# Adding the residual of row tiles 0 to 7 with accumulating stores from GpSimd onto rows that already hold x

## The chip, the cores and the metric

The kernel runs on one core of one Trainium2 chip. The time is the device time of one execution in microseconds, as the median of several runs. A profile is one further execution with the hardware profiler on; its span runs from the first to the last instruction.

The core's engines run their own instruction queues and wait for one another through semaphores: TensorE (PE, matmuls into the PSUM banks), VectorE (DVE), ScalarE (ACT), GpSimd (POOL) and SyncE (SP, which here issues every DMA). DMAs move data between the device memory (HBM) and the on-chip memory (SBUF).

## What is computed

One transformer block on x of 2048 rows and 512 columns in bfloat16, with the attention and the gated MLP side by side:

```
xn  = layernorm(x)
q, k, v = split(xn @ wqkv)                  # 32 heads of 16
att: each row attends to itself and rows -2, -4, ... -14   (8 positions, dilation 2)
A   = softmax(q.k / 4) . v  ->  @ wo
B   = (gelu(xn @ w_gate) * (xn @ w_up)) @ w_down            # inner width 1376
out = x + A + B
```

The last line matters here: x, the residual, is added to the sum of the two branches.

## The kernel before

The rows are cut into 4 blocks (b = 0 to 3) of 512 rows, and each block into 4 row tiles of 128 rows, so that there are 16 row tiles t. Names carry these numbers: `pr2_1` is work of block 2, `fe7` work of row tile 7.

For each block, in the order of the data:

- The row tiles are loaded (`ld_x`), normalised (`norm`) and transposed into xnT: block 0 by PE, the others by DMA transposes from SP (`trx`).
- PE computes q, k and v (`mm<b>_<q|k|v>_<group>`, L1009; block 0's q and k in smaller pieces) and ACT evicts them (`ev`).
- DVE multiplies q with the eight shifted views of k (`pr`, 128 x 4096 elements each) and adds pairs (`pa`). PE sums over the head's columns (`er`, L1085). DVE and ACT do the softmax (`d1`, `d2`, `exp`, `d4` to `d6`). The probabilities go to HBM and come back replicated over partitions (`ss`, then `sl` into PT, L1176). DVE multiplies them with v (`pv`), adds (`pw`) and writes the attention's output (`pz`, L1199).
- PE computes the gate and up products (`fg`, `fu`, L1217), ACT applies gelu (`gelu`) and evicts (`uev`), DVE multiplies the two (`h`).
- For each row tile, PE accumulates attention output times Wo and MLP inner times Wd in one PSUM bank (`acc`, L1302).

Then comes the part that is changed. For row tiles 0 to 13, ACT evicts the bank into one of four slots of the buffer OB (`fe`, L1335), DVE adds x in place from one of two slots of XR (`fin`, L1340), and SP stores the slot to the output (`sto`, L1353). SP loads XR beforehand (`ldxr`, L1288). Row tiles 14 and 15 are cut into two and three pieces, and DVE adds x straight from PSUM (L1346).

The order on every engine is written out by hand: `ORDER` holds one list of task names per engine. `schedule` assigns the buffer slots along these lists, with a model of durations, and `assign_sync` derives the semaphore waits. No engine leaves its list: an instruction that waits holds everything behind it. A slot of OB is free when the DMA that read it has landed, and the next `fe` that takes that slot waits for it on ACT. The last stores on SP are preceded by waits for all earlier DMAs. GpSimd has only constants to write, and four small powers for the normalisation (`sq8` to `sq14`, L832).

Of the kernel before, what the change touches and what calls it, by code (L numbers as in the profile page):

```python
# [12 lines left out]
    DMA_ISSUE=0.48,  # L13
    DMA_FIXED=2.0,
# [5 lines left out]
    DRAIN=0.1,  # L20
# [115 lines left out]
class Graph:  # L136
# [70 lines left out]
    def schedule(self, orders, params=None):  # L207
        prm = dict(PARAMS)
# [58 lines left out]
        for _ in range(len(self.tasks)):  # L267
# [23 lines left out]
            elif t.eng == "pe":  # L291
                sw = 0.0
                if t.mode is not None:
                    if pe_mode not in (None, t.mode):
                        sw = prm["PE_MODE_SWITCH"]
                    pe_mode = t.mode
                t.end = est + sw + pe_clock.run(est, t.dur, t.util)
                t.done = t.end + prm["PE_DRAIN"]
            else:
                t.end = est + t.dur  # L300
                t.done = t.end + prm["DRAIN"]
                if t.eng == "act" and t.table is not None:
                    act_table = t.table
# [13 lines left out]
    def assign_sync(self, cnt_sems, dma_sems):  # L317
        order = self.order
        for e in ("pe", "act", "dve", "pool"):
            for i, t in enumerate(order[e]):  # L320
                t.seq = i + 1
                t.sem = cnt_sems[e]
                t.val = i + 1
        dcount = [0] * len(dma_sems)
        dlast = [None] * len(dma_sems)
        k = 0
        for t in order["sp"]:
# [6 lines left out]
            dlast[si] = t  # L334
        self.dma_totals = [(dma_sems[i], dcount[i]) for i in range(len(dma_sems)) if dcount[i] > 0]
        know = {e: {} for e in ENGS}
        allt = sorted((t for t in self.tasks if not t.dropped), key=lambda t: (t.start, t.idx))
        for t in allt:
            K = know[t.eng]
            deps = list(t.deps)  # L340
            if t.eng == "sp" and t.prev_on_sem is not None:
                deps.append(t.prev_on_sem)
# [21 lines left out]
    def emit_engine(self, eng_name, e):  # L364
# [7 lines left out]
        for t in self.order[eng_name]:  # L372
# [10 lines left out]
            ins.then_inc(t.sem, 16 if eng_name == "sp" else 1)  # L383
# [5 lines left out]
    def report(self):  # L389
# [30 lines left out]
    "act":  # L420
        "c_tbl sx1 sq0 negm1 sxx1 sq1 evx0_0 evx0_1 evq0_0 sq2 evq0_1 evk0_0 evx1_0 sq3 evk0_1 bnst8 evx1_1 "
        "bnst9 evq0_2 sq6 evk0_2 evq0_3 evk0_3 ve8 evv0_0_0 sq4 vp8 bnag8 bnag9 va8 gelu0_0 evv0_2_0 "
        "evv0_3_0 bnst10 gelu0_1 bnst11 uev0_2 gelu0_3 vb8 gelu0_4 uev0_1 uev0_3 ve10 gelu0_5 uev0_4 uev0_0 "
        "uev0_5 gelu0_2 halo1 vp10 gelu0_7 bnag10 bnag11 evq1_0_0 evk1_0_0 evv0_1_0 evq1_1_0 evk1_1_0 "
        "gelu0_6 exp0 sub11 evq1_3_0 evk1_3_0 evq1_2_0 va10 uev0_7 uev1_0 uev0_10c uev0_6 sub9 vb10 sub8 "
        "uev1_1 evk1_2_0 norm9 uev0_10b gelu1_1 gelu1_0 norm8 gelu0_8 evv1_0_0 gelu1_2 sub10 uev0_8 bnst12 "
        "gelu0_9 norm11 uev1_2 uev0_9 norm10 evv1_2_0 gelu1_4 gelu1_3 uev1_3 evv1_1_0 uev1_4 uev1_5 uev0_10a "
        "bnst13 gelu1_5 gelu0_10 uev1_6 evk2_1_0 evv1_3_0 evk2_0_0 ve12 vp12 gelu1_7 bnag12 evq2_0_0 gelu1_6 "
        "evq2_1_0 uev1_10b bnag13 uev1_10c halv1 evk2_2_0 evq2_2_0 halo2 exp1 bnst14 sub12 bnst15 uev1_7 "
        "va12 ve14 vb12 uev1_10a vp14 bnag14 evk2_3_0 bnag15 evq2_3_0 evv2_1_0 va14 vb14 fe1 fe2 sub14 "  # L430
        "gelu2_0 evv2_2_0 halo3 gelu1_10 sub15 uev2_0 norm12 sub13 evv2_0_0 evv2_3_0 norm13 fe0 norm15 fe3 "
        "norm14 gelu1_8 gelu2_1 gelu1_9 uev2_1 uev1_8 uev2_2 uev1_9 uev2_3 gelu2_2 evk3_2_0 evk3_1_0 "
        "uev2_10b gelu2_3 exp2 evq3_1_0 evk3_3_0 evq3_2_0 evq3_0_0 halv2 evk3_0_0 uev2_10c evq3_3_0 uev2_4 "
        "uev2_10a gelu2_10 gelu3_1 uev3_0 gelu3_0 fe7 evv3_0_0 gelu2_5 gelu3_3 evv3_1_0 uev2_5 uev3_1 fe5 "
        "gelu2_4 gelu3_2 uev3_10c halv3 evv3_3_0 uev3_2 fe4 fe6 uev3_3 uev3_10b exp3 gelu3_5 uev2_6 gelu3_4 "
        "gelu2_7 uev2_7 uev2_8 gelu3_6 gelu2_6 evv3_2_0 gelu3_7 uev3_4 gelu2_8 gelu2_9 uev2_9 uev3_10a "
        "uev3_7 uev3_5 uev3_6 gelu3_10 fe10 gelu3_8 gelu3_9 uev3_9 fe9 uev3_8 fe8 fe11 fe13 fe12",
    "dve":
        "c_wdz bnst0 bnag0 sub0 rstd0 norm0 mean1 sub1 evy0_0 rstd1 norm1 evy0_1 bnst2 bnag2 sub2 rstd2 "
        "norm2 bnst3 bnag3 sub3 rstd3 norm3 bnst7 bnst6 bnst5 bnag6 bnag7 bnst4 bnag5 sub7 rstd6 bnag4 sub6 "  # L440
        "norm7 sub4 sub5 norm6 pr0_2 pr0_0 pr0_3 rstd4 pr0_1 norm4 norm5 pa0_1 pa0_0 h0_0 h0_1 h0_2 mask "
        "d1_0 d2_0 pr1_0 pr1_1 d4a_0 d4b_0 d4c_0 d5_0 rstd8 d6_0 pr1_3 pa1_0 pr1_2 h0_3 pa1_1 pv0_1 rstd10 "
        "pv0_3 h0_4 pv0_0 h1_1 pv0_2 pw0_1 h0_10 pw0_2 d1_1 pw0_3 d2_1 pz0 pr2_2 d4a_1 pr2_0 d4b_1 h1_3 "
# [12 lines left out]
        "ss0_1 ldxr2 sl0_1 sl0_3 sl0_2 trx4_0 sl0_0 trx4_1 trx5_1 trx5_0 ss1_2 ss1_3 ss1_1 ss1_0 sl1_1 sl1_3 "
        "sl1_0 sl1_2 ldxr3 trx6_0 trx6_1 trx7_1 trx7_0 sto3 sto1 ldxr0 ldxr7 ss2_1 ss2_2 ss2_3 ss2_0 sl2_0 "
        "sl2_3 sl2_2 sto0 sl2_1 sto2 ldxr5 ldxr4 sto5 ss3_0 ss3_1 ss3_2 ss3_3 ldxr10 sl3_3 sl3_0 sl3_2 sl3_1 "
        "ldxr6 sto4 sto6 ldxr8 ldxr9 sto9 ldxr11 ldxr14 sto8 sto7 sto10 ldxr13 sto11 sto14_0 sto14_1 ldxr15 "
        "ldxr12 sto13 sto15_0 sto15_1 sto12 sto15_2",  # L460
# [20 lines left out]
def bass_parallel_sum__sliding_local_dilated__glu_gated_geglu__prompt_kernel(nc, A_x, A_wqkv, A_wo, B_x, B_w_gate, B_w_up, B_w_down, out, dbg=None, cfg=None):  # L481
# [28 lines left out]
    PPOW = cfg.get("PPOW", 4)  # L510
    FIN2 = cfg.get("FIN2", tuple(range(14)))
# [12 lines left out]
    with contextlib.ExitStack() as es:  # L524
# [56 lines left out]
        cnt = {e: es.enter_context(nc.semaphore("cnt_" + e)) for e in ("pe", "act", "dve", "pool")}  # L581
        dsems = [es.enter_context(nc.semaphore("dma%d" % i)) for i in range(NDMASEM)]
# [360 lines left out]
        for b in range(NB):  # L943
# [338 lines left out]

            for ti in range(4):
                t = 4 * b + ti
                it_xr = Item("xr%d" % t, P_xr, "xr")

                def mk_xr(t=t, it=it_xr):
                    return lambda e: e.dma_start(XR[:, it.slot, :], x2[128 * t:128 * t + 128, :])  # L1288
                t_xr = G.task("sp", "ldxr%d" % t, 0, mk_xr(), wr=[it_xr], prio=base + 58, nbytes=128 * 1024)
                G.order_after(t_xr, t_of["gelu%d_5" % b])  # L1290
                cparts = TAIL_SPLIT.get(t, [(0, 512)])
                for ci, (c0, c1) in enumerate(cparts):
# [40 lines left out]
                    if t in FIN2:  # L1333
# [4 lines left out]

                        def mk_fin(itx=it_xr, ito=it_ob):
# [14 lines left out]
                    G.task("sp", "sto" + sfx, 0, mk_so(), rd=[it_ob], wr=[(I_out, (t, ci))], prio=base + 62,  # L1354
# [11 lines left out]
        G.assign_sync(cnt, dsems)  # L1366
# [50 lines left out]
```

## Time and profile before

| what | value |
| --- | --- |
| median of 5 runs | 184.15 us (183.92 to 184.55) |
| the profiled execution: time, span | 183.92 us, 182.1 us |
| matmuls of 512 columns (L1217), four in a row | 0.86 us |
| DVE, 128 x 4096 elements (L1040) | 2284 ns, 16 of them |
| DVE, `fin` (L1340) | 14 of them, 5.7 us in all |
| ACT, `fe` (L1335) | 14 of them, 600 ns each |
| POOL, power (L832) | 4 of them, 866 to 6880 ns |
| `ldxr` (L1288): issue to landing, median | 2.2 us, 128 KB each |
| `sto` (L1353) of 128 KB: issue to landing, median | 2.0 us |

The time of an execution is its span and the little that lies around it, here 1.8 us. An engine's busy time and share of the span are given by the profile's first part; "idle before" is the time an engine stood still ahead of an instruction, with what ended it. Lines are given as L and a number, and belong to the kernel before. A duration in the profile can be longer than the step to the next instruction of the same engine, as neighbours overlap at their ends.

### The profile page before, as it was taken

To read this page: it belongs to the slowest core of one execution; us is meant where nothing else is said; L and a number is where in the kernel's file an instruction comes from. 1 tells how busy PE (TensorE), PEld (TensorE's weight loads), DVE (VectorE), ACT (ScalarE), POOL (GpSimd) and SP (SyncE) were. 2 spreads that over 40 slices of the span, in tenths; PEclk is the share of its full clock that TensorE was granted. 3 is DMA by queue.
4 is the path that set the end of the run, shared out by engine and by line. 5 is a ranking of instruction groups with operands and counts; after the bars stand their busy time and mean duration, and the time that the engine had idled before them with its cause. 6 is when DMAs were issued, how large, how long until landed. Compare 5 with 4: busy or idle time off the path is not lost.

```text
span 182.1 us, 2773 instructions
## 1 busy us (share of the span) xinstructions
PE 177.5 (97%) x1051; PEld 90.4 (50%) x1068; DVE 169.6 (93%) x172; ACT 128.4 (71%) x258; POOL 15.7 (9%) x23
## 2 busy tenths in 40 slices
PE   8999999999999999999999999999999999999994
PEld 2895444544444544444444544444444444444664
DVE  3779999999999999999999999999999999999922
ACT  5789977999998999997795977437449664234011
POOL 6000049004200000131000000000000000000000
PEclk9999999999999999999999999999999999999999
DMA  4999925932562000003861020127200355022433
GB/s 137 363 376 380 118 31 128 363 110 59 193 126 58 0 0 0 4 17 81 250 60 30 25 61 0 32 59 237 79 0 0 95 152 191 0 86 59 146 94 107
DMA packets 26220, 19.60 MB, mean 108 GB/s; under 512 B 13824, under 2 KB 23008, under 8 KB 26208
## 3 DMA queue, kind: packets, MB, share of 16 engines
q1 hardware_dynamic: 26208, 19.44, 37.7%
q8 instruction: 8, 0.13, 0.3%
q14 instruction: 4, 0.03, 0.1%
HBM read 14.71 MB, written 3.15 MB: 98 GB/s over the span
## 4 chain that ended last, share of the span: by engine, by line
PE 95%; DMA 1%; issue 1%; ACT 1%; DVE 0%; SPq 0%; DVEq 0%
PE PS L1217 38%; PE PS L1302 28%; PE PS L1009 19%; PE PS L959 4%; PE PS L1256 2%; PE PS L1085 2%; PE PS L1078 1%; DMA XIN<-in_A_x_dram 1%; PE PS L899 1%; ACT KT L986 0%; ACT xnT L919 0%; PE PS L678 0%; SPq L731 0%; DVE XIN L873 0%; DVE OB L1346 0%
## 5 line engine op out<-in xcount | busy, mean ns | idle before, releaser
L1302 PE MATMUL PS<-Wd,HT 128*128 128x512 bf16 (+2 forms) x206 | 40.7, 345 | 0.3 <-issue 0.2
L1217 PE MATMUL PS<-xnT,Wg 128*128 128x512 bf16 x156 | 39.0, 379 | 0.2
L1217 PE MATMUL PS<-xnT,Wu 128*128 128x512 bf16 x156 | 38.9, 379 | 0.2
L1009 PE MATMUL PS<-xnT,Wqkv 128*128 128x512 bf16 x155 | 37.2, 379 | 0.4 <-issue 0.2
L1184 DVE TENSOR_TENSOR UNI<-VN,PT 128x4096 f16<-128x4096 bf16 x16 | 36.2, 2281 | 0.0
L1040 DVE TENSOR_TENSOR UNI<-QT,KT 128x4096 f16<-128x4096 bf16 x16 | 36.1, 2284 | 0.0
L1302 PEld LDWEIGHTS PS<-Wd,HT 128*128 128x128 bf16 x209 | 19.5, 98 | 19.2 <-issue 0.4
L1234 ACT ACTIVATE UU<-PS 128x512 bf16<-128x512 f32 x40 | 23.1, 599 | 6.6 <-PE PS L1217 6.3
L1193 DVE TENSOR_TENSOR UNI<-UNI 128x4096 f16<-128x4096 f16 x12 | 27.4, 2284 | 0.0
L1227 ACT ACTIVATE GG<-PS 128x512 bf16<-128x512 f32 x40 | 22.9, 601 | 5.6 <-DVE HT L1241 5.5
L1009 PEld LDWEIGHTS PS<-xnT,Wqkv 128*128 128x128 bf16 x160 | 17.9, 113 | 16.9 <-issue 0.8
L1217 PEld LDWEIGHTS PS<-xnT,Wu 128*128 128x128 bf16 x160 | 15.6, 98 | 19.0 <-ACT XIN L853 0.4
L1217 PEld LDWEIGHTS PS<-xnT,Wg 128*128 128x128 bf16 x160 | 15.7, 98 | 18.7
L1335 ACT ACTIVATE OB<-PS 128x512 bf16<-128x512 f32 x14 | 8.3, 600 | 17.3 <-PE PS L1302 15.1
L832 POOL TENSOR_TENSOR sq<-ve,mhalf 128x2 bf16<-128x2 f32 x4 | 12.8, 3200 | 66.0 <-ACT ve L828 66.0
L1053 DVE TENSOR_TENSOR UNI<-UNI 128x4096 f16<-128x4096 f16 x8 | 18.2, 2282 | 0.0
L1302 PE MATMUL PS<-Wo,OT 128*128 128x512 bf16 (+2 forms) x75 | 16.4, 345 | 0.1
L1020 ACT ACTIVATE VN<-PS 128x512 bf16<-128x512 f32 x16 | 9.3, 596 | 6.5 <-PE PS L1009 6.5
L1241 DVE TENSOR_TENSOR HT<-GG,UU 128x1024 bf16<-128x1024 bf16 x20 | 13.5, 682 | 0.0
L1302 PEld LDWEIGHTS PS<-Wo,OT 128*128 128x128 bf16 x76 | 7.1, 98 | 6.6 <-issue 0.3
L1272 ACT ACTIVATE UT<-PS 64x256 bf16<-64x256 f32 (+1 forms) x12 | 5.4, 448 | 6.7 <-PE PS L1256 3.9
L959 PE MATMUL PS<-xnT,Wqkv 128*128 128x128 bf16 x128 | 8.0, 219 | 0.1
(85 smaller groups left out, 159.1 us busy)
## 6 DMA issues: line engine op xcount, KB each, us to landing
PT<-pt_scratch SPq DMA_DIRECT2D x16, 256.0 KB, 4.1
XR<-in_A_x_dram SPq DMA_DIRECT2D x16, 128.0 KB, 2.2
out_dram<-OB SPq DMA_DIRECT2D x14, 128.0 KB, 2.0
Wqkv<-in_A_wqkv_dram SPq DMA_DIRECT2D x3, 512.0 KB, 4.8
XIN<-in_A_x_dram SPq DMA_DIRECT2D x6, 256.0 KB, 6.3
Wg<-in_B_w_gate_dram SPq DMA_DIRECT2D x1, 1280.0 KB, 8.8
Wu<-in_B_w_up_dram SPq DMA_DIRECT2D x1, 1280.0 KB, 11.7
Wd<-in_B_w_down_dram SPq DMA_DIRECT2D x1, 1280.0 KB, 6.3
```

Of the source, the lines that this page charges most:

```text
L832: "pool", "sq%d" % t, 7.0, lambda e, t=t, n=n: e.tensor_tensor(out=sq[:, t:t + n], in0=ve[:, t:t + n], in1=mhalf[:, 0:n], op=ALU.pow),
L959: ins = e.matmul(PS[:, 512 * it.slot + 128 * g:512 * it.slot + 128 * g + 128], lhsT=wcols(which, kt, g), rhs=xnT[:, itx.slot, kt, t * 128: ...
L1009: ins = e.matmul(PS[:, 512 * it.slot:512 * it.slot + 512], lhsT=wcols(which, kt, g), rhs=xnT[:, itx.slot, kt, :], start=(kt == 0), stop=(k ...
L1040: return lambda e: e.tensor_tensor(out=UNI[:, it.slot, :, :], in0=bass.AP(QT, (itq.slot * 4 + g) * 512, [[NQT * 4 * 512, 128], [0, 8], [1, ...
L1053: return lambda e: e.tensor_tensor(out=UNI[:, i0.slot, :, :], in0=UNI[:, i0.slot, :, :], in1=UNI[:, i1.slot, :, :], op=ALU.add)
L1184: return lambda e: e.tensor_tensor(out=bass.AP(UNI, ito.slot * 4096, [[NUNI * 4096, 128], [2048, 2], [512, 4], [1, 512]]), in0=bass.AP(VN, ...
L1193: return lambda e: e.tensor_tensor(out=UNI[:, i0.slot, :, :], in0=UNI[:, i0.slot, :, :], in1=UNI[:, i1.slot, :, :], op=ALU.add)
L1217: ins = e.matmul(PS[0:M, 512 * it.slot:512 * it.slot + 512], lhsT=Wx[:, kt, j * 128:j * 128 + M], rhs=xnT[:, itx.slot, kt, :], start=(kt = ...
L1227: return lambda e: e.activation(out=GG[:, ito.slot, q, :], in_=PS[:, 512 * it.slot:512 * it.slot + 512], func=ACTF.Gelu_apprx_tanh)
L1234: return lambda e: e.activation(out=UU[:, ito.slot, q, :], in_=PS[:, 512 * it.slot:512 * it.slot + 512], func=ACTF.Identity)
L1241: return lambda e: e.tensor_tensor(out=HT[:, ito.slot, j - 1:j + 1, :], in0=GG[:, ig.slot, :, :], in1=UU[:, iu.slot, :, :], op=ALU.mult)
L1302: ins = e.matmul(PS[:, 512 * it.slot:512 * it.slot + CW], lhsT=(OT[:, ito.slot, q, ti * 128:(ti + 1) * 128] if kind == "o" else HT[:, ith. ...
```

## The change

For row tiles 0 to 7 (blocks 0 and 1), neither `ldxr` nor `fin` nor `sto` is left. Instead:

- SP copies the block's 512 rows of x from HBM to the output in HBM in one DMA (`prx0`, `prx1`, 512 KB each). Like `ldxr` before, it waits for the block's sixth gelu (`gelu0_5`, `gelu1_5`).
- ACT evicts the bank into OB as before (`fe`).
- GpSimd issues a DMA that adds the OB slot onto the rows of the output (`sta`, 128 KB each). It waits for `fe` and for the block's `prx`. The model that assigns the slots takes 4 us of GpSimd and 3 us to landing for it.

The `sta` DMAs have six semaphores of their own; SP waits for these too before the last four stores. Row tiles 8 to 15 are treated as before. All five lists of `ORDER` but for their beginnings are new.

The diff (of the lists, those of SP and POOL, the new ones of DVE and PE, and the new end of ACT's):

```diff
+    POOL_DMA=3.0,
...
-                t.done = t.end + prm["DRAIN"]
+                t.done = t.end + (prm["POOL_DMA"] if t.nbytes else prm["DRAIN"])
...
-            for i, t in enumerate(order[e]):
+            for i, t in enumerate(q for q in order[e] if not (e == "pool" and q.nbytes)):
...
+        last = [None] * len(acc_sems)
+        for k, t in enumerate(q for q in order["pool"] if q.nbytes):
+            i = k % len(acc_sems)
+            t.sem = acc_sems[i]
+            t.val = 16 * (k // len(acc_sems) + 1)
+            t.prev_on_sem = last[i]
+            last[i] = t
+        self.acc_last = [t for t in last if t is not None]
...
             if eng_name == "sp" and t is self.order["sp"][-4]:
                 late = self.order["sp"][-7:]
+                for q in self.acc_last:
+                    e.wait_ge(q.sem, q.val)
...
     "pe":
...
+        "mm0_2_1_0 mm0_2_2_0 mm0_2_0_0 fg0_0 fg0_1 fg0_2 fg0_3 fu0_0 fu0_1 fg0_4 fu0_2 fu0_3 fg0_5 fu0_4 "
+        "fu0_5 fg0_6 fg0_7 mm0_2_3_0 er0_3 mm1_1_0_0 mm1_0_0_0 mm1_0_1_0 mm1_1_1_0 mm1_0_2_0 mm1_1_2_0 "
...
+        "mm2_2_2_0 accd1 mm2_1_3_0 fu2_0 fg1_8 accd2 fg2_1 fg1_9 mm2_2_0_0 acca0 fg1_10 fg2_2 fu1_8 accb0 "
+        "mm2_2_3_0 fu2_1 fu2_2 accd3 fg2_3 fg2_10 fu2_3 er2_3 fu1_9 mm3_1_0_0 mm3_0_0_0 mm3_1_1_0 mm3_1_3_0 "
+        "mm3_2_0_0 mm3_0_2_0 mm3_1_2_0 mm3_0_1_0 mm3_0_3_0 fg2_4 mm3_2_2_0 fg3_0 fu2_4 fg3_1 fg2_5 acca4 "
+        "fu3_0 accd5 fu3_1 accb4 fg3_2 mm3_2_3_0 fu2_5 accd7 er3_3 fg3_3 fg2_6 fu3_2 fu3_3 accd6 fg2_7 fg3_4 "
...
+        "fg3_9 fu3_7 fu3_8 fu3_9 acca8 accd10 accb8 accd11 accd9 acca12 accd14_0 accd13 accd14_1 accw14_0 "
+        "accw14_1 accw13 accd15_0 accw15_0 accb12 accw12 accd15_1 accw15_1 accd15_2 accw15_2",
     "act":
...
+        "evq3_1_0 uev2_4 evv3_2_0 evv3_0_0 gelu2_10 gelu2_4 gelu2_5 uev3_0 fe4 uev2_5 gelu3_0 fe5 gelu3_2 "
+        "gelu3_1 uev3_1 evv3_3_0 fe7 uev3_3 gelu3_3 uev3_10b uev3_10c exp3 fe6 uev3_2 uev2_6 gelu2_6 gelu2_7 "
+        "gelu3_4 uev3_4 evv3_1_0 uev2_7 uev3_5 gelu3_5 uev2_8 uev2_9 gelu2_9 gelu2_8 gelu3_6 gelu3_7 gelu3_8 "
+        "uev3_10a halv3 gelu3_9 uev3_6 uev3_8 uev3_7 uev3_9 gelu3_10 fe8 fe10 fe9 fe11 fe13 fe12",
     "dve":
...
+        "norm2 bnst3 bnag3 sub3 rstd3 norm3 bnst4 bnst7 bnst6 bnag4 bnag7 bnst5 bnag6 sub4 sub7 bnag5 sub6 "
+        "rstd6 sub5 norm6 norm7 pr0_2 pr0_0 rstd4 pr0_1 norm5 norm4 pr0_3 pa0_0 pa0_1 h0_1 h0_2 h0_0 mask "
+        "d1_0 d2_0 pr1_0 pr1_1 d4a_0 d4b_0 d4c_0 d5_0 d6_0 pa1_0 rstd8 pr1_2 pr1_3 h0_3 pa1_1 pv0_3 rstd10 "
+        "pv0_1 h0_4 pv0_0 pv0_2 h1_1 pw0_1 h0_10 pw0_2 d1_1 pw0_3 d2_1 pz0 pr2_1 d4a_1 pr2_2 d4b_1 pr2_0 "
+        "d4c_1 d5_1 d6_1 h1_3 pr2_3 h1_0 h1_2 pa2_1 rstd12 pa2_0 pv1_1 rstd14 pv1_0 pv1_2 h1_10 pw1_1 pv1_3 "
+        "d1_2 pw1_2 d2_2 pw1_3 h2_1 d4a_2 h1_4 d4b_2 pz1 d4c_2 pr3_3 d5_2 pr3_0 d6_2 pr3_2 h2_0 pa3_1 pr3_1 "
+        "h2_10 pa3_0 pv2_1 d1_3 pv2_2 d2_3 pv2_3 pv2_0 d4a_3 h2_2 d4b_3 h3_1 d4c_3 d5_3 pw2_1 d6_3 pw2_2 "
+        "h3_2 h3_0 pw2_3 h2_4 h2_3 pz2 pv3_1 pv3_0 pv3_2 h3_4 pw3_1 fin8 pw3_2 h3_3 h3_10 fin10 pv3_3 fin9 "
+        "pw3_3 fin11 pz3 fin14_0 fin14_1 fin13 fin15_0 fin15_1 fin12 fin15_2",
     "pool":
-        "c_utz sq8 sq10 sq12 sq14",
+        "c_utz sq8 sq10 sq12 sq14 sta0 sta3 sta2 sta5 sta7 sta4 sta1 sta6",
     "sp":
-        "ld_x0_0 ld_x0_1 ld_wq ld_x1_0 ld_wk ld_x1_1 ld_wv ld_x2 ld_x4 ld_x3 ld_wg0 ld_wu0 ld_wt0 ld_x5 "
-        "ld_wt1 trx3_0 ld_wt2 trx3_1 trx2_0 trx2_1 ld_wd0 ld_x6 ldxr1 ld_x7 ld_wd1 ld_wo ss0_2 ss0_3 ss0_0 "
-        "ss0_1 ldxr2 sl0_1 sl0_3 sl0_2 trx4_0 sl0_0 trx4_1 trx5_1 trx5_0 ss1_2 ss1_3 ss1_1 ss1_0 sl1_1 sl1_3 "
-        "sl1_0 sl1_2 ldxr3 trx6_0 trx6_1 trx7_1 trx7_0 sto3 sto1 ldxr0 ldxr7 ss2_1 ss2_2 ss2_3 ss2_0 sl2_0 "
-        "sl2_3 sl2_2 sto0 sl2_1 sto2 ldxr5 ldxr4 sto5 ss3_0 ss3_1 ss3_2 ss3_3 ldxr10 sl3_3 sl3_0 sl3_2 sl3_1 "
-        "ldxr6 sto4 sto6 ldxr8 ldxr9 sto9 ldxr11 ldxr14 sto8 sto7 sto10 ldxr13 sto11 sto14_0 sto14_1 ldxr15 "
-        "ldxr12 sto13 sto15_0 sto15_1 sto12 sto15_2",
+        "ld_x0_0 ld_x0_1 ld_wq ld_x1_0 ld_wk ld_x1_1 ld_wv ld_x2 ld_x4 ld_x3 ld_wg0 ld_wu0 ld_x5 ld_wt0 "
+        "ld_wt1 trx3_0 ld_wt2 trx3_1 trx2_0 ld_x7 trx2_1 prx0 ld_wd0 ld_wd1 ld_wo ld_x6 ss0_0 ss0_1 ss0_2 "
+        "ss0_3 sl0_3 sl0_1 sl0_2 sl0_0 trx4_1 trx4_0 trx5_0 trx5_1 ss1_0 ss1_1 ss1_3 ss1_2 sl1_1 sl1_2 sl1_0 "
+        "sl1_3 trx6_1 trx6_0 trx7_0 trx7_1 prx1 ss2_1 ss2_3 ss2_0 ss2_2 sl2_1 sl2_3 sl2_2 sl2_0 ldxr10 ldxr8 "
+        "ss3_1 ss3_3 ss3_2 ss3_0 sl3_1 sl3_3 sl3_0 sl3_2 ldxr9 sto8 ldxr11 sto9 sto10 ldxr14 sto11 ldxr13 "
+        "sto14_0 ldxr15 sto14_1 ldxr12 sto13 sto15_0 sto15_1 sto12 sto15_2",
...
+    FIN3 = cfg.get("FIN3", tuple(range(8)))
...
+        asems = [es.enter_context(nc.semaphore("acc%d" % i)) for i in range(6)]
...
+            if 4 * b in FIN3:
+                def mk_px(b=b):
+                    return lambda e: e.dma_start(out2[512 * b:512 * b + 512, :], x2[512 * b:512 * b + 512, :])
+                t_px = G.task("sp", "prx%d" % b, 0, mk_px(), wr=[(I_out, b)], prio=base + 58, nbytes=512 * 1024)
+                G.order_after(t_px, t_of["gelu%d_5" % b])
...
+                        if t in FIN3:
+                            def mk_ao(t=t, ito=it_ob):
+                                return lambda e: e.dma_start(out2[128 * t:128 * t + 128, :], OB[:, ito.slot, :],
+                                                             accum_op=ALU.add)
+                            G.task("pool", "sta%d" % t, 4.0, mk_ao(), rd=[it_ob, (I_out, t // 4)], prio=base + 62,
+                                   nbytes=128 * 1024)
+                            continue
...
-        G.assign_sync(cnt, dsems)
+        G.assign_sync(cnt, dsems, asems)
```

## The prediction

> **What bounds the kernel now.** I read the head of the page and its busy times first, then the chain that ended last, then PE's own waits and its busy time by stage, and last the rows of what the change touches. From the page:
>
> ```profile
> span 182.1 us, 2773 instructions
> PE 177.5 (97%) x1051; PEld 90.4 (50%) x1068; DVE 169.6 (93%) x172; ACT 128.4 (71%) x258; POOL 15.7 (9%) x23
> ...
> PE 95%; DMA 1%; issue 1%; ACT 1%; DVE 0%; SPq 0%; DVEq 0%
> ```
>
> TensorE carries 95% of the chain. The stages (length, then PE busy) and everything PE itself waited for, from the windows and from PE's waits:
>
> ```profile
> 5.00:60.00 55.00, 54.51 (x381) 30.56 (x387) 52.78 (x66) 49.35 (x107) 9.72 (x2) 1.00 0.66 188
> 60.00:120.00 60.00, 59.63 (x323) 28.40 (x328) 59.60 (x49) 48.80 (x98) 3.08 (x2) 1.00 0.19 45
> 120.00:172.00 52.00, 51.68 (x270) 24.29 (x273) 51.98 (x46) 26.08 (x47) 0.00 (x0) 1.00 0.29 92
> ```
>
> ```profile
> PE PS L678 <- PEq L1402: 0.8, 1, 0.8
> PE PS L1009 <- issue: 0.2, 1, 0.2
> PE PS L1302 <- issue: 0.2, 1, 0.2
> ```
>
> Between 5 and 172 us PE is idle for 167 - 165.82 = 1.2 us in all, at a granted clock of 1.00, and never for another engine. The head (5 us) and the tail (last matmul ends at 179.58, span 182.1) are fixed by a load, the first normalisation, and a last addition and store. So whatever DVE sheds, the floor is at most 1.2 us below.
>
> DVE is nearly the second bound (52.0 of the last 52 us), and its margin is thinnest at the end. In DVE's timeline pz3 (L1199) is the last work of block 3 that PE needs:
>
> ```profile
> 168.83 2.28 DVE L1193 TENSOR_TENSOR UNI<-UNI 128x4096 f16<-128x4096 f16 x1
> 171.03 0.42 DVE L1340 TENSOR_TENSOR OB<-OB,XR 128x512 bf16<-128x512 bf16 x1
> 171.37 1.22 DVE L1199 TENSOR_TENSOR OT<-UNI 128x2048 bf16<-128x2048 f16 x1
> ```
>
> It ends at 172.59; its consumer accw14_0 starts at about 173.1. Half a microsecond of DVE delay there would reach PE.
>
> **The change part by part.**
>
> *Removed from DVE:* eight of the fourteen L1340 additions (fin0 to fin7). One is 0.42 us long but costs 0.34 us from start to start (171.03 to 171.37): 8 x 0.34 = 2.7 us. Nothing of it is on the chain. It becomes DVE margin.
>
> *The new order.* I put both orders on the trace's clock by adding rows. PE: from 14.52 us (first 512-column projection), 0.216 us for each 512-column matmul (four take 0.86), 1.5 us for an er group. For before this ends at 179.65 against 179.58 measured. The matmuls are the same, so after ends there too unless PE waits. DVE: from 15.97 us, 2.20 us for each 4096-element operation, 0.61 for 1024, 0.34 for 512, 1.14 for pz. This is up to 1.2 us late at the end of before (pz3 at 172.58 by the sum, 171.37 measured), so the margins err on the cautious side. Margin of PE's need over DVE's end, before and after: pa0 to er0 0.26 and 0.26; pz0 to accd1 0.54 and 0.54; pa2 to er2 3.2 and 8.7; pa3 to er3 0.73 and 0.78; pz1 to block 1's first Wo matmul 1.5 and 2.7; pz2 to acca8 -0.3 and 1.95; pz3 to accw14_0 -0.5 and 2.2. None gets worse. ACT runs at 71%; laying its order out with 0.49 us per eviction and 1.28 per table load, the tightest PSUM bank after is exp2's before mm3_2_2 (0.5 us; before, evictions at about 0.5 to 0.6). Cost 0; the cover is these margins.
>
> *Moved on SP:* 100 DMAs become 86: sixteen (eight ldxr, eight sto) go, two prx come. prx0 waits for gelu0_5, and ld_wd0, ld_wd1, ld_wo, ld_x6 and ss0 now stand behind it. gelu0_5 is done by about 27 us (before, ldxr1 had the same wait and was issued at 30.0); Wd is first needed at 71.9 us (accd1), and took 6.3 us to land. prx0 moves 512 KB in and out; at the 363 GB/s of slice 8, 1.05 MB is 2.9 us. Wd then lands by about 40 us: 0, hidden by 30 us. ss0 is issued when d6_0 is done (41.3 us by the sum, 41.5 before). prx1 waits only behind the transposes (issued until 96 us before) and is needed by sta5 at about 125 us.
>
> *fg0_0 comes 0.86 us earlier* (17.11 by the sum, before 17.8 measured and 17.97 by the sum). Its Wg landed 8.8 us after issue at 7.56, that is at 16.4 us; 0.6 us of margin. Cost 0, at most some tenths.
>
> *Added on POOL:* eight accumulating stores, two waits for prx. No row of before shows a DMA issued by POOL. POOL's own rows and the SP store it replaces:
>
> ```profile
> L832 POOL TENSOR_TENSOR sq<-ve,mhalf x4: 866/2528/6880, 25.4 to 80.4; 128x2 bf16<-128x2 f32 x4
> ```
>
> ```profile
> L1353 SPq DMA_DIRECT2D out_dram<-OB x19: 332/429/578, 103.5 to 180.0; - x19
> ...
> DMA to landing us min/median/max: 1.5/1.8/4.4
> ```
>
> Issue costs between 0.33 us (the shortest SP store) and 6.88 us (a POOL operation on two elements a partition, held for three DVE operations). Landing takes between 1.5 us and, since an addition reads and writes HBM, twice the longest, 8.8 us. I take 2.5 + 4.4 = 7 us: POOL's median row, as it is the same engine beside the same DVE, and the slow store. Who waits: the four OB slots. fe4, fe5 and fe7 (121.5, 125 and 127.5 us) need sta0, sta3 and sta2, whose fe0 and fe3 end near 92.6 and 95.9: over 20 us. fe6 (136.1) needs sta5, which starts after fe5 (125.5): 10.6 us, the tightest. fe8 (160) needs sta7 (from 128); fe10, fe9 and fe11 have as much. All hidden at 7 us; also at 6.88 us of issue each with landings of 3 us. At 6.88 + 8.8 = 15.7 us fe6 would be 5 us late, and with it every eviction queued behind it on ACT.
>
> The POOL row is also where the Trainium skill speaks against the change. SBUF — State Buffer (Summary: rules for kernel authors) says to issue from ACT or SP a DMA that is to hide under DVE work, as descriptor writing on GpSimd starves while DVE runs a fast mode; its section Who interferes with whom narrows that: an operation with two SBUF inputs, which is almost all of DVE's work here, blocks only GpSimd's reads. By its example (620 ns becomes 3100) a store costs 2.5 us more, which the OB margins also hide; the sum would be the same. The trace shows the reads blocked (6.88 us) and shows no descriptor writing.
>
> *The tail* keeps its order: fin15_1 at 178.84, fin12 at 179.05, fin15_2 at 179.68, then sto12 and sto15_2. fin15_0 is no longer held behind a late accd15_0. The six added semaphore waits stand before sto15_0, about 1 us earlier than before; sto15_0 followed fin15_0 by 0.1 us with some seventeen such waits, so 0.
>
> **Sum.** 183.92 (profiled execution: 182.1 of span and 1.8 around) + 0 = 183.9. The median of the five runs, 184.15, is 0.23 higher. As the thin margins at pz2 and pz3 widen, I expect some of that to go: 184.0.
>
> **Rivals.**
>
> 1. *GpSimd holds DVE off (slower).* If writing descriptors keeps DVE from its second SBUF input, each store costs DVE x. It decides from 8x > 2.7 + 0.5, x = 0.4 us; at x = 0.87 (POOL's shortest row) PE is late by 7.0 - 3.2 = 3.8 us: 187.9. Against it: in before, DVE lost nothing beside POOL's four operations (its 4096-element operations stay at 2281 to 2284 ns, idle 0.0).
>
> 2. *A transfer is late in the new order (slower).* Wg for fg0_0; PT for pv1_1, which has 0.65 us less after d6_1 than before (d6_1 0.4 later, pv1_1 0.25 earlier) and whose loads take 3.2 to 5.1 us; PT of block 2, beside sta5 and sta7; PT of block 3, which has 8.0 us after d6_3 where before had 9.2. A lateness of 1 to 3 us less up to 2 us of DVE margin leaves 0.4 to 1.5 us: 184.9.
>
> 3. *OB slots come late (slower).* From 10.6 us for sta5 on. At the upper bound 5 us, less about 1 us of free PSUM banks: 188.
>
> 4. *Faster.* If what lifts the typical run of before above its profiled one is DVE's missing margin, and one or two of PE's 0.2 us issue gaps fall away with the new neighbours of er0 and er3: 183.92 - 0.3 = 183.6.
>
> **How the numbers follow.** No change 0.47; rival 4 0.16; rival 2 0.22; rival 1 0.09; rival 3 0.06. About 0.2% (0.37 us) is what a measurement of this kernel can tell from no change, so faster is below 183.78 and slower above 184.52: faster 0.16, same 0.47, slower 0.37. The likeliest case alone spans 183.8 to 184.5. The range of 183.5 to 186.5 leaves out rivals 1 and 3 and a little of rival 4.
>
> **What would show it.** Right: PE still has no wait for an engine or a DMA; DVE busy falls by 8 x 0.42 = 3.4 us to about 166.2 and its new idle time stands before operations that wait for PT, ACT or PE; pz3 ends some 2.5 us earlier; ACT's fe rows wait for PE only; the tail repeats. Wrong: PE waiting for ACT near fe6 (rival 3), DVE operations longer or idle beside POOL's DMAs (rival 1), a gap on PE at 17 us or DVE waiting for PT above 2 us (rival 2). The forecast fails most easily if POOL-issued stores disturb something that no row of before could show.

## The result, and the profile after

The changed kernel takes 184.89 us (median of 21 runs, 184.48 to 186.16) against 184.29 us of the kernel before on the same chip (41 runs, 183.92 to 185.28). The ratio is 1.0032, with a 95% interval of 1.0022 to 1.0043. It is slower, by a third of a percent, where no change was forecast.

The head of the page of the changed kernel, and its chain by engine:

```profile
span 182.6 us, 2764 instructions
PE 177.1 (97%) x1051; PEld 90.2 (49%) x1068; DVE 167.8 (92%) x164; ACT 127.8 (70%) x258; POOL 14.2 (8%) x31
...
PE 89%; DMA 4%; ACT 3%; SPq 2%; issue 1%; DVE 0%; DVEq 0%; ACTq 0%
```

PE still bounds it, but its share of the chain fell from 95% to 89%, and a transfer and ACT have come in. Where they stand is seen in the chain of waits itself (start, length, what). The changed kernel, from 5 us on:

```profile
4.78 6.56 DMA XIN<-in_A_x_dram
11.34 0.02 issue
11.36 0.72 ACT XS L780 x2
12.08 0.48 ACT KT L997
12.57 0.50 ACT xnT L930
13.06 0.05 issue
13.11 1.98 PE PS L970 x32
15.09 0.05 issue
15.14 2.54 PE PS L1020 x11
```

The kernel before over the same stretch (lines of code after the change stand 11 to 25 higher: L769 is now L780, L919 L930, L959 L970, L986 L997, L1009 L1020):

```profile
10.48 1.08 PE PS L959 x16
11.57 0.22 PE PS L899 x4
11.79 2.68 PE PS L959 x48
...
14.52 3.40 PE PS L1009 x15
```

The first projection of 512 columns begins at 15.14 instead of 14.52 us. The last matmul ends at 180.18 instead of 179.58. From the one to the other it is 165.04 us after and 165.06 before: everything behind 15 us, where the residual is, takes the same time in PE's queue. The 0.6 us by which the last matmul ends later in this pair of profiles are lost between 11 and 13 us, in the first block's projections, some 70 us ahead of the first residual row.

ACT's timeline shows how (start, length, line, what; in brackets the idle time before it and what ended that). After:

```profile
11.36 0.63 ACT L780 ACTIVATE XS<-XIN 128x512 bf16<-128x512 bf16 x1 [0.93 <-DMA XIN<-in_A_x_dram]
...
11.99 0.58 ACT L997 ACTIVATE KT<-PS 128x512 bf16<-128x512 f32 x1
12.47 0.59 ACT L930 ACTIVATE xnT<-PS 128x512 bf16<-128x512 bf16 x1
```

Before:

```profile
10.50 0.60 ACT L986 ACTIVATE KT<-PS 128x512 bf16<-128x512 f32 x1
10.97 0.64 ACT L769 ACTIVATE XS<-XIN 128x512 bf16<-128x512 bf16 x1
...
11.83 0.60 ACT L919 ACTIVATE xnT<-PS 128x512 bf16<-128x512 bf16 x1
```

The new list of ACT has two tasks of the head exchanged. Before, it reads `sq3 evk0_1 bnst8 evx1_1`, after, `sq3 bnst8 evk0_1 evx1_1`. bnst8 is the row sum of tile 8 (L780), which belongs to block 2 and is wanted at leisure. It needs the load of x4, and x4 lands at 11.34 us. So ACT stands for 0.93 us, and behind it stand evk0_1, the eviction of a piece of k, and evx1_1, the eviction of the transposed x that PE's next matmuls read. In the profile before, x4 landed at 10.9 us (issued at 4.77, 6.2 us to landing), 0.4 us sooner behind the same loads. PE now waits 0.6 us for that xnT. Past the first loads its other waits for an engine come to 0.2 us, for ACT at 100 us; the 0.4 us for Wqkv in this view stand at 6 us, among the first loads, and e1 below has 0.3 us of them too:

```profile
PE PS L970 <- ACT xnT L930: 0.6, 1, 0.6
PE PS L970 <- DMA Wqkv<-in_A_wqkv_dram: 0.4, 1, 0.4
PE PS L1020 <- issue: 0.2, 1, 0.2
```

The windows of 12 to 15 us (length; busy time of PE, PEld, DVE, ACT, POOL; granted clock, DMA share, GB/s), after and then before, say the same: PE 2.39 of 3.00 us against 2.95, at the same clock and the same DMA rate.

```profile
12.00:15.00 3.00, 2.39 (x41) 2.24 (x41) 2.90 (x11) 3.00 (x9) 0.00 (x0) 1.00 1.03 391
```

```profile
12.00:15.00 3.00, 2.95 (x48) 2.69 (x47) 3.00 (x12) 2.77 (x8) 0.00 (x0) 1.00 1.03 396
```

The part that the change is named for behaves well. The stores on POOL, from the views of OB and of the DMAs (KB each, median us from issue to landing), and the only wait of the `fe` rows:

```profile
L1358 POOL DMA_DIRECT2D out_dram<-OB x8: 837/959/1504, 93.8 to 137.8; - x8
```

```profile
out_dram<-OB POOLq DMA_DIRECT2D x8, 128.0 KB, 3.8
out_dram<-in_A_x_dram SPq DMA_DIRECT2D x2, 512.0 KB, 5.0
```

```profile
ACT OB L1352 <- PE PS L1319: 26.0, 6, 7.4
```

A store costs POOL 0.84 to 1.50 us and lands 3.8 us after its issue. No `fe` waits for a slot of OB. And DVE's last work of block 3 for PE, pz3, now at L1210, is followed by 2.40 us of idle time, where before 1.21 us followed it:

```profile
170.78 1.22 DVE L1210 TENSOR_TENSOR OT<-UNI 128x2048 bf16<-128x2048 f16 x1
174.40 0.83 DVE L1371 TENSOR_TENSOR OB<-PS,XR 128x256 bf16<-128x256 f32 x2 [2.40 <-PE PS L1319]
```

There is a second, smaller part. The time of an execution less its span was 1.8 us in the profile before. Over all runs of the changed kernel it is 2.11 us (2.06 to 2.17), over the 35 runs of the kernel before in the second set below 1.87 us (1.81 to 1.93). So of the 0.60 us between the medians, 0.24 lie outside the span and 0.36 inside. What follows explains the part inside; the cause of the other stays open.

### The profile page after: what moved, and what is told of

Its sections match the earlier page's. It is cut to its first block, busy times and chain, and to the rows that moved or that the text cites. A ratio compares the mean times of both kernels' runs of the same rounds, so it can differ in the third digit from the quotient of the medians.

```text
span 182.6 us, 2764 instructions
## 1 busy us (share of the span) xinstructions
PE 177.1 (97%) x1051; PEld 90.2 (49%) x1068; DVE 167.8 (92%) x164; ACT 127.8 (70%) x258; POOL 14.2 (8%) x31
## 4 chain that ended last, share of the span: by engine, by line
PE 89%; DMA 4%; ACT 3%; SPq 2%; issue 1%; DVE 0%; DVEq 0%; ACTq 0%
PE PS L1228 37%; PE PS L1319 28%; PE PS L1020 18%; DMA XIN<-in_A_x_dram 4%; PE PS L1267 2%; PE PS L1096 1%; PE PS L970 1%; SPq L742 1%; PE PS L1089 1%; SPq L698 1%; ACT GG L1238 1%; ACT UT L1283 1%; ACT XS L780 0%; ACT KT L1031 0%; ACT QT L1031 0%
## 5 line engine op out<-in xcount | busy, mean ns | idle before, releaser
L1228 PE MATMUL PS<-xnT,Wu 128*128 128x512 bf16 x158 | 38.3, 379 | 0.3 <-ACT UU L1245 0.2
L1228 PE MATMUL PS<-xnT,Wg 128*128 128x512 bf16 x154 | 38.1, 379 | 0.4 <-issue 0.2
L1020 PE MATMUL PS<-xnT,Wqkv 128*128 128x512 bf16 x155 | 36.4, 379 | 0.4 <-issue 0.2
L1195 DVE TENSOR_TENSOR UNI<-VN,PT 128x4096 f16<-128x4096 bf16 x16 | 36.1, 2283 | 0.2 <-ACT VN L1039 0.2
L1245 ACT ACTIVATE UU<-PS 128x512 bf16<-128x512 f32 x40 | 23.5, 606 | 13.0 <-PE PS L1228 10.9
L1204 DVE TENSOR_TENSOR UNI<-UNI 128x4096 f16<-128x4096 f16 x12 | 27.3, 2278 | 0.0
L1020 PEld LDWEIGHTS PS<-xnT,Wqkv 128*128 128x128 bf16 x160 | 17.9, 114 | 16.8 <-ACT GG L1238 0.4
L1064 DVE TENSOR_TENSOR UNI<-UNI 128x4096 f16<-128x4096 f16 x8 | 18.2, 2283 | 0.0
L1358 POOL DMA_DIRECT2D out_dram<-OB x8 | 7.1, 1042 | 47.1 <-ACT GG L1238 28.2
L843 POOL TENSOR_TENSOR sq<-ve,mhalf 128x2 bf16<-128x2 f32 x4 | 4.2, 1054 | 76.5 <-ACT ve L839 76.5
L970 PE MATMUL PS<-xnT,Wqkv 128*128 128x128 bf16 x128 | 8.2, 219 | 1.0 <-ACT xnT L930 0.6
```

The source lines that it names most:

```text
L970: ins = e.matmul(PS[:, 512 * it.slot + 128 * g:512 * it.slot + 128 * g + 128], lhsT=wcols(which, kt, g), rhs=xnT[:, itx.slot, kt, t * 128: ...
L1020: ins = e.matmul(PS[:, 512 * it.slot:512 * it.slot + 512], lhsT=wcols(which, kt, g), rhs=xnT[:, itx.slot, kt, :], start=(kt == 0), stop=(k ...
L1064: return lambda e: e.tensor_tensor(out=UNI[:, i0.slot, :, :], in0=UNI[:, i0.slot, :, :], in1=UNI[:, i1.slot, :, :], op=ALU.add)
L1195: return lambda e: e.tensor_tensor(out=bass.AP(UNI, ito.slot * 4096, [[NUNI * 4096, 128], [2048, 2], [512, 4], [1, 512]]), in0=bass.AP(VN, ...
L1204: return lambda e: e.tensor_tensor(out=UNI[:, i0.slot, :, :], in0=UNI[:, i0.slot, :, :], in1=UNI[:, i1.slot, :, :], op=ALU.add)
L1228: ins = e.matmul(PS[0:M, 512 * it.slot:512 * it.slot + 512], lhsT=Wx[:, kt, j * 128:j * 128 + M], rhs=xnT[:, itx.slot, kt, :], start=(kt = ...
```

## The experiments

The theory after the traces: the exchange of bnst8 and evk0_1 puts PE behind x4's landing, and the residual's move is worth nothing either way. The rivals: the loss sits elsewhere in the new lists; or the accumulating stores and the copies of x cost it; or the freed DVE time gains something that the head's loss hides.

Each set of runs had its own runs of the kernel before on the same chip: 184.47 us in the first set, 184.48 in the second, 184.32 in the third.

**First set: the exchange undone, made alone, and its cause taken away in two ways.**

*e1*, the changed kernel with the two tasks put back:

```diff
-evx1_0 sq3 bnst8 evk0_1 evx1_1
+evx1_0 sq3 evk0_1 bnst8 evx1_1
```

> The changed kernel with one swap on ACT: bnst8 (the row sum that waits for the load of x4) goes back behind evk0_1, as before the change. Theory (the whole loss is made between 11 and 13 us, where bnst8 holds evk0_1 and evx1_1 on ACT): the first 512-column matmul moves from 15.14 back to about 14.5 us, PE's wait of 0.61 us for ACT xnT is gone, the time falls by 0.6 us to 184.3, ratio to before 1.000 (0.998 to 1.001). Rival (the stores from GpSimd, the copies from HBM to HBM or the rest of the new order cost it): the ratio stays near 1.003 and the time near 184.9.

Measured: 184.22 us (183.95 to 184.69), ratio 0.9985 [0.9971, 0.9998]. The chain in the head:

```profile
11.33 0.72 ACT XS L780 x2
12.05 0.49 ACT xnT L930
...
12.59 1.98 PE PS L970 x32
14.57 2.59 PE PS L1020 x12
```

x4 landed at the same time (11.30 us), but evk0_1 was done by then, and PE's 32 matmuls start at 12.59 instead of 13.11. The last matmul ends at 179.67, 0.51 us before that of the changed kernel and 0.09 us after that of the kernel before: at this landing of x4 the exchange costs 0.5 us. Two words in one list are worth more than the whole difference between the two kernels.

*e2*, the kernel before with the exchange alone:

```diff
-evx1_0 sq3 evk0_1 bnst8 evx1_1
+evx1_0 sq3 bnst8 evk0_1 evx1_1
```

> The kernel before with the same swap the other way: bnst8 ahead of evk0_1, nothing else. Theory: PE waits about 0.6 us for ACT near 12.5 us, and since DVE and ACT follow PE's shift the end is 0.5 to 0.7 us later: 184.9, ratio 1.003. Rival: within 0.1% of before, as the swap is only two ACT instructions.

Measured: 184.69 us (184.21 to 185.18), ratio 1.0007 [0.9993, 1.0021]. The profile has the same wait, `PE PS L959 <- ACT xnT L919`, of 0.8 us, and a first 512-column projection at 15.32 us, but the median rose by only 0.22 us: by time alone this run is inconclusive. e5 and e9 below offer a reason, which no run tests by itself: the kernel before is late for its loads in many runs, so that part of this price is already in its median.

*e3*, the changed kernel with x4 loaded ahead of the V weights (`ld_x4 ld_wv ld_x2 ld_x3`; the plan's rule that x4 is loaded behind these weights is lifted for it, as in e8 to e10):

> The changed kernel with its ACT order left as it is, but the load of x4 issued one place earlier, before the load of Wv (512 KB, some 1.4 us at the 365 GB/s of the head). Theory: it is the landing of x4 (11.34 us) that bnst8 waits for; with x4 some 1 to 1.4 us earlier ACT's wait of 0.93 us is gone, and with it most of the 0.6 us: 184.3 to 184.5, ratio 1.000 to 1.001. If it were the ACT time of bnst8 itself (0.63 us ahead of evk0_1), the time would stay at 184.9. The rival on the stores also says 184.9.

*e4*, the changed kernel with bnst8 and bnst9 moved four and five places later on ACT, behind the evictions (`sq3 evk0_1 evx1_1 evq0_2 evk0_2 bnst8 sq6 evq0_3 evk0_3 bnst9 sq4`):

> The changed kernel with bnst8 and bnst9 behind all evictions that PE needs for block 0's q and k up to its third row tile (order evk0_1 evx1_1 evq0_2 evk0_2 bnst8 sq6 evq0_3 evk0_3 bnst9 sq4). Theory: in the order of before, bnst8 still stands ahead of evx1_1 with no margin to the landing of x4 (it starts at 10.97 us, x4 lands at about 11); taking both off the chain makes the head independent of that landing. As fast as the swap alone or up to 0.2 us faster, 184.1 to 184.3, with a narrower spread, ratio 0.999 to 1.000. If the head has no such dependence left after the swap: equal to the swap. If bnst9 so late delays the normalisation of block 2: no, rows 8 and 9 are needed 30 us later.

Measured: 184.11 us, ratio 0.9982 [0.9969, 0.9996], and 184.22 us, ratio 0.9982 [0.9967, 0.9998]. The first 512-column projection begins at 14.30 and 14.47 us. Either way of taking x4 out from in front of the evictions wins 0.6 to 0.8 us back from the changed kernel (184.89, and 184.80 when measured again below), and all three mended kernels are a little below the kernel before.

**Second set: a dose, and the other parts.**

The changed kernel once more, unaltered:

> The changed kernel once more, as the yardstick for the others of its batch. Expected: 0.3% over the kernel before (ratio between 1.0015 and 1.0045), with the row sum of x4 standing ahead of the eviction evk0_1 on ScalarE and waiting for x4, which lands at 11.3 to 11.6 us, and the first 512-column projection at 15.1 to 15.4 us. If another chip or another batch makes the ratio 1.000, the loss measured first was no property of the kernel.

Measured: 184.80 us (184.29 to 185.48), ratio 1.0017 [0.9994, 1.004]; in this set the kernel before had four runs near 186 us, which widens the interval. The profiled execution is of use, since x4 came later in it:

```profile
12.10 0.63 ACT L780 ACTIVATE XS<-XIN 128x512 bf16<-128x512 bf16 x1 [1.30 <-DMA XIN<-in_A_x_dram]
```

*e7*, the changed kernel with x4 loaded one place later:

```diff
-ld_x2 ld_x4 ld_x3
+ld_x2 ld_x3 ld_x4
```

> The changed kernel with one more swap: on SP's queue x3 is loaded before x4, so that x4 lands later by the time of one 256 KB load, some 0.65 us at the 390 GB/s of these slices; nothing else is changed. Theory (evk0_1 and evx1_1 stand behind x4): x4 lands at about 12.0 us, the first 512-column projection begins at about 15.8 us, and the time grows by about 0.65 us over the changed kernel, to 185.5 us. Rival (the 0.6 us come from another part of the new lists): no change, 184.9 us.

Measured: 185.62 us (185.09 to 185.94), ratio 1.0051 [1.0024, 1.0078], 0.8 us over the changed kernel of the same set. Its chain:

```profile
6.78 5.33 DMA XIN<-in_A_x_dram
...
12.13 0.72 ACT XS L780 x2
...
13.88 1.98 PE PS L970 x32
...
15.91 2.54 PE PS L1020 x11
```

With these three executions of one ACT list the landing of x4 can be set against the time:

| execution | x4 lands | first 512-column projection | last matmul ends | time |
| --- | --- | --- | --- | --- |
| changed kernel, first profile | 11.34 | 15.14 | 180.18 | 184.77 |
| changed kernel, second profile | 12.08 | 15.88 | 180.92 | 185.48 |
| e7 | 12.10 | 15.91 | 180.95 | 185.52 |

The projection follows the landing by 3.80 or 3.81 us, and 165.04 us later the last matmul ends. From 11.34 to 12.08 the time grows by 0.71 for 0.74 us. In these executions, which are three at two different landings, the landing of one load that block 2 needs sets the time of the kernel, one for one.

*e5*, the kernel before with both row sums late (two and five places):

```diff
-sq3 evk0_1 bnst8 evx1_1 bnst9 evq0_2 sq6 evk0_2 evq0_3 evk0_3 ve8 evv0_0_0 sq4
+sq3 evk0_1 evx1_1 evq0_2 bnst8 sq6 evk0_2 evq0_3 evk0_3 bnst9 ve8 evv0_0_0 sq4
```

> The kernel before with the row sums bnst8 and bnst9 moved three and four places later on ScalarE, so that no eviction of the head stands behind x4; the residual stays on VectorE. Theory (x4's landing in front of the evictions is the whole loss, and the residual's move is worth nothing): as the changed kernel with the same late row sums, 184.1 to 184.2 us, and 0.1 to 0.3 us below the kernel before, because there too bnst8 stands ahead of evx1_1 and pays whenever x4 lands after 11.1 us; first 512-column projection at 14.5 us. Rival (the freed VectorE time is what made the mended kernels 0.25 to 0.36 us faster than the one before): no faster than the kernel before, 184.4 to 184.5 us.

Measured: 184.68 us (183.99 to 185.08), ratio 0.9996 [0.9969, 1.0023]. By its time it sides with the rival. Its profiled execution is one of its fastest (184.08 us), so that no trace shows what made the median; but it names a third thing, from DVE's and then PE's timeline:

```profile
11.78 1.88 DVE L750 BATCH_NORM_STATS2 st<-XIN 128x6 f32<-128x512 bf16 x3 [0.76 <-DMA XIN<-in_A_x_dram]
...
25.46 4.48 DVE L1053 TENSOR_TENSOR UNI<-UNI 128x4096 f16<-128x4096 f16 x2
```

```profile
30.09 0.62 PE L1078 MATMUL PS<-xnT,Wt 128*32 128x256 bf16 x16 [0.25 <-DVE UNI L1053]
```

From the landing of x3, for which the first of the three statistics waits, DVE works without a gap until 29.94, and PE waits 0.25 us for it. In the profile of before the same DVE work ends at 29.86 and PE's matmuls start at 29.96: 0.1 us of room. The kernel before thus has an exposure of its own to a late load, on another engine. In the new lists DVE does the statistics of tile 4 while x3 is still under way, so that less is left for afterwards: in e1, with the wait for x3 over at 12.07 us, later than here, DVE ends at 29.63 and PE's matmuls start at 30.04, 0.4 us of room.

*e6*, the mended kernel e1 with the residual of tiles 0 to 7 put back on DVE by hand, as plain stores with XR loads (eight `fin`, `ldxr` and `sto` in; `sta` and `prx` out):

```diff
-pa2_1 rstd12 pa2_0 pv1_1 ... pv1_2 h1_10 pw1_1 pv1_3 d1_2
+pa2_1 fin2 rstd12 pa2_0 fin1 pv1_1 ... pv1_2 fin0 h1_10 pw1_1 pv1_3 fin3 d1_2
...
-pa3_0 pv2_1 d1_3 pv2_2 d2_3 pv2_3 pv2_0 d4a_3 h2_2
+pa3_0 fin4 pv2_1 fin5 d1_3 pv2_2 fin7 d2_3 pv2_3 pv2_0 d4a_3 fin6 h2_2
```

> The changed kernel's lists with ScalarE's head as before (evk0_1 ahead of bnst8), and the residual of tiles 0 to 7 back on VectorE: eight final adds, their eight loads of x and eight plain stores put into the new lists by hand, no accumulating store and no copy of x. It does the whole computation. Theory (the residual's move is worth nothing while PE is the bound): equal to the same lists with the accumulating stores, 184.2 us (184.0 to 184.5). Rival (2.7 us less on VectorE is worth something, or the accumulating stores cost something): above 184.5 us, or below 183.9 us.

Measured: 184.98 us (184.59 to 185.57), ratio 1.0024 [1.0002, 1.0046], against the theory. The head is fast (first 512-column projection at 14.41), but the last matmul ends 165.95 us later instead of 165.04 (165.10 in e1). From its waits between 120 and 146 us, and DVE's timeline there:

```profile
ACT UU L1245 <- DVE HT L1252: 3.0, 1, 3.0
...
PE PS L1020 <- ACT GG L1238: 0.7, 1, 0.7
```

```profile
139.30 0.42 DVE L1365 TENSOR_TENSOR OB<-OB,XR 128x512 bf16<-128x512 bf16 x1
139.64 0.68 DVE L1252 TENSOR_TENSOR HT<-GG,UU 128x1024 bf16<-128x1024 bf16 x1
```

Four additions stand between 126 and 140 us ahead of one gate product (HT), four times 0.34 us. ACT waits for that product's buffer, and PE for ACT. So the freed time on DVE had been spent: the new order has no room for the additions at these places, although the old order has them all at no cost to PE. The run shows that additions at these places cost PE time in this order; it does not show that the residual's move is worth that time, since the old order carries the same additions elsewhere. That needed the cleaner edit below.

**Third set: the loads out of the way, and the residual alone.**

Three kernels have the 512 KB load of the V weights, first read at 14.3 us, moved behind x2, x4 and x3 on SP, so that none of these is late:

```diff
-ld_x1_1 ld_wv ld_x2 ld_x4 ld_x3
+ld_x1_1 ld_x2 ld_x4 ld_x3 ld_wv
```

*e8*, the changed kernel so, with ACT's exchange left in:

> The changed kernel with the 512 KB load of the V weights moved behind x2, x4 and x3 on SP's queue, so that these three land 1.3 us (512 KB at 390 GB/s) sooner; ScalarE's order stays as changed, bnst8 ahead of evk0_1. The V weights land at about 12 us and are first read at 14.3 us. Theory (the loss is the landing of x4 in front of the evictions and nothing else): first 512-column projection at 14.3 us, 184.05 us (183.9 to 184.4), and runs closer together than those of the kernel before, since neither x4 nor x3 is waited for any more. Rival (ScalarE's order costs something by itself): 184.5 us or more.

Measured: 184.04 us (183.94 to 184.22), ratio 0.9984 [0.9975, 0.9994]. bnst8 starts without a wait, and PE has no wait for xnT:

```profile
10.36 0.63 ACT L780 ACTIVATE XS<-XIN 128x512 bf16<-128x512 bf16 x1
...
10.97 0.60 ACT L997 ACTIVATE KT<-PS 128x512 bf16<-128x512 f32 x1
11.69 0.60 ACT L930 ACTIVATE xnT<-PS 128x512 bf16<-128x512 bf16 x1
```

With x4 early the exchange costs nothing. The 12 runs lie within 0.3 us of each other, those of the unaltered one within 1.2 (12 runs) and 1.7 (21): most of its spread went with the late landing of these three loads. With x4 alone out of the way (e3) it was 0.7.

*e9*, the kernel before so:

> The kernel before with the same move of the V weights' load; its residual and all else stay. Theory (x3 and x4 landing late is what spreads the runs of the kernel before between 183.9 and 186.1 us: bnst8 stands ahead of evx1_1, and VectorE's chain from x3 to the first score block has 0.1 us of room): 184.0 to 184.1 us with runs within 0.6 us of each other, 0.3 to 0.4 us below the kernel before, and equal to the changed kernel with the same move within 0.1 us. Rival (the residual's move gains something of its own): 0.2 us or more above that one.

Measured: 183.93 us (183.63 to 184.65), ratio 0.9977 [0.9963, 0.999]: median as expected, spread 1.0 us rather than 0.6. The kernel before, too, gains 0.4 us from loads that come in time, and the two kernels so mended are 0.1 us apart, the old one ahead. Inside the span the changed one is ahead, by the medians 181.95 us against 182.1; it loses that by the 0.23 us more that lie outside its span.

*e10*, the old lists with the same loads, and in them the residual alone exchanged (`fin`, `ldxr`, `sto` of tiles 0 to 7 out, `sta` in the order of the `fe` on POOL and two `prx` on SP in), nothing planned anew:

> The lists of the kernel before, with the same move of the V weights' load, and in them only the residual of tiles 0 to 7 exchanged: eight final adds, eight loads of x and eight plain stores out, eight accumulating stores on POOL's queue and two copies of x in. Nothing else is planned anew. Theory (the residual's move by itself is worth nothing): equal to the kernel before with the moved load within 0.1 us, 184.0 to 184.1 us, the stretch from the first 512-column projection to the last matmul 165.05 us as there. Rivals: 0.2 us or more below it (the freed 2.7 us of VectorE count), or 0.2 us or more above it (the accumulating stores hold something up).

*e11*, the same exchange with the loads in their old order:

> The same exchange of the residual alone, in the lists of the kernel before with its loads in their old order. Theory (the 0.6 us come from the new lists and not from the residual): as the kernel before within 0.1 us, 184.4 to 184.5 us, with its spread. Rival (the accumulating stores or the copies of x cost the 0.6 us): 184.9 us or more, ratio 1.002 to 1.004.

Measured: e10 183.76 us (183.53 to 184.25), ratio 0.9968 [0.9951, 0.9984], which beats both kernels, mostly by the moved load; e11 184.11 us (183.86 to 184.60), ratio 0.9987 [0.9976, 0.9999]. e10 is 0.17 us below e9, e11 0.21 us below its kernel before: somewhat more than the 0.1 us that was expected, though the interval of e11 only just excludes no change, and the runs of e9 and e10 spread over 0.7 us and more. Of these, 0.12 and 0.14 us lie outside the span: e10 and e11 have 1.74 and 1.72 us there, the kernels they came from 1.86. Inside, the medians of the spans, given to 0.1 us, are 0.1 us lower each. PE's stretch, from the chains of e9 and then e10 (the first 512-column projection, and the last piece of PE):

```profile
14.51 3.45 PE PS L1009 x16
...
162.86 16.75 PE PS L1302 x122
```

```profile
14.96 3.45 PE PS L1022 x16
...
163.30 16.75 PE PS L1321 x122
```

In the profile of e10 the last matmul ends 165.09 us after the first 512-column projection, in that of e9 165.10. In that of e11 it is 165.26; there x3 is waited for until 11.80 us, DVE's last work for PE's sums ends at 29.95, and PE starts them at 30.05, much as in e5. So for PE the residual's move is worth nothing that these runs can tell, and it costs nothing either. e10's profiled execution, at 184.25 us the slowest of its runs, has a late head although x2, x4 and x3 are early: the weights of k landed at 8.66 us, and PE waited 0.5 us for them. Loads ahead of the moved ones can spread the runs too.

Not settled is what makes the time outside the span: 1.87 us for the old lists, 2.08 to 2.11 for the changed kernel and every variant of it with accumulating stores (e1, e3, e4, e7, e8), 1.75 for e6, 1.72 to 1.74 for e10 and e11. Within a program it varies by less than 0.1 us either way. The residual's exchange alone lowers it by 0.12 to 0.14 us in the old lists and raises it by 0.33 in the new ones (from e6 to e1), so it follows neither the lists nor the stores alone, and the traces show nothing there.

## Why the prediction was wrong, point by point

*What fails: the cost of the new order was put at 0, from sums that begin at 14.52 us; ahead of that PE's list was taken as unchanged in time.* The sums started "PE: from 14.52 us (first 512-column projection)", "DVE: from 15.97 us", and the head counted as "fixed by a load, the first normalisation". That PE's head has the same matmuls is true. But ACT's list changes at its fifteenth task, at 10.5 us, and PE's head hangs on ACT's evictions. Read from the profile of before, the exchange could have been priced: x4 landed there at 10.9 us, in time for bnst8 at 10.97 but not for 10.50, where the new list wants it. Moved ahead of evk0_1, bnst8 waits until x4 is there, and bnst8's 0.63 us and evk0_1's 0.48 (from start to start) then stand in front of evx1_1, which ran at 11.83. With x4 landing at 10.93 us evx1_1 starts at 12.06, a loss of 0.2 us; with x4 at 11.34, at 12.47, a loss of 0.64 us, and 12.47 is what the profile after shows. That x4 lands anywhere from 10.9 to 12.08 us in different executions could not be read from one profile.

*"Between 5 and 172 us PE ... never for another engine", the bound and its floor:* right. All that could be lost or won was small, and PE's stretch past 14.5 us repeated within 0.02 us.

*The time around the span as 1.8 us:* wrong for the changed kernel, 2.11. This is 0.24 of the 0.60 us; it could not be read from any row of before, and its cause is open.

*Eight additions off DVE as margin with no gain:* right for PE. Its size on the far end was less than said: DVE's busy time fell by 1.8 us to 167.8, not to about 166.2, and pz3's room grew by 1.2 us (idle time behind it 1.21 to 2.40), not by 2.5. The 3.4 us of the prediction count the ends at which neighbours overlap; by its own 0.34 us from start to start it is 2.7. e11, which exchanges the residual alone, has 167.6 us, so the rest is not the new lists' doing; its cause was not found. Among DVE's new idle times are 0.7 us each for ACT's exponentials and for an XR load.

*POOL's stores at 2.5 + 4.4 = 7 us:* the mechanism was right, both terms too large: 0.96 us of issue at the median and 3.8 us of landing. The page of the Trainium skill cited there, SBUF — State Buffer, in its section Who interferes with whom, held up where its summary did not: beside DVE operations that are nearly all two-input ones the issue stayed within 0.84 to 1.50 us. No run shows it with DVE at rest.

*SP's move at 0:* right. prx0's 512 KB took 5.0 us, where the sum had 2.9; Wd's landing grew from 6.3 to 8.9 us, and PE waited for neither. *Wg's 0.6 us of margin* held: PE had no wait at 17 us.

*Rival 1, DVE held off:* refuted; its 4096-element operations stay at 2278 to 2283 ns. *Rival 3, slots of OB late:* refuted; the `fe` rows wait for PE alone. *Rival 4, faster:* half of its reason was seen. The kernel before does lie above its profiled execution for a cause inside it, but 0.4 us of it are loads that come late (e9), and taking DVE's additions away gave PE nothing (e10).

*Rival 2, a transfer is late in the new order, at 184.9 us:* this is the case that came about, at its time, but with a transfer that was not on its list. Wg and the PT loads were checked because DVE and PE wait for them; x4 was not, because the task that waits for it is on ACT, in a stretch that the sums left out. That the time agrees is chance: the rival's 0.9 us came from other transfers, and 0.24 of the measured 0.60 us lie outside the span.

## What to carry to other kernels

When an order is planned anew, compare every engine's list from its first line, and for each task that moved earlier ask when its input lands, which the profile tells by the load's issue and its time to landing, for one execution. A task of a later block that waits for a load does not belong in front of evictions that PE waits for, and a load whose consumer is urgent belongs ahead of a larger one whose consumer is not. And a spread between runs of the same kernel is worth a look: here loads that land late made most of it in the changed kernel and some of it in the one before, and one load moved took 0.4 us off the kernel before and 0.8 off the changed one.

## What the runs showed of the hardware

The 256 KB load of x4, behind the same loads, landed between 10.9 us (before) and 12.08 us (second profile of the changed kernel) in profiled executions that had it at the same place in the queue. A DMA of 128 KB from SBUF that GpSimd issues and that adds to rows in HBM took 0.84 to 1.50 us of the engine and 3.8 us to land, against 0.33 to 0.58 us and 2.0 us for a plain store from SP; a copy of 512 KB from HBM to HBM took 5.0 us. And GpSimd's power on two elements per partition (L843), 0.87 to 6.88 us before, took 0.69 to 2.03 us after, where the new order has it beside other DVE operations.
